# Four durations in the planner of an attention and expert kernel, set to recorded ones

## The chip, the core and the metric

The kernel runs on one core of a Trainium2 chip. The metric is the device time of one execution in microseconds; the time before is the median of three runs. Engines are named as in the profile: PE is TensorE (PEld its weight loads), DVE is VectorE, ACT is ScalarE, POOL is GpSimd, SP is the engine whose queue issues the DMAs.

## What is computed

Rotary attention over 4 x 8 heads of 576 positions with 64 features, then a gated feed-forward layer over the 2304 tokens that come out of it:

```python
q_rot, k_rot = rotate(q), rotate(k)
scores = q_rot @ k_rot.T / sqrt(64)          # per head, 576 x 576
attn = softmax(scores)
x = (attn @ v), as 2304 tokens x 512
xn = x / sqrt(mean(x * x) + 1e-6) * rms_g
h = silu(xn @ w_gate) * (xn @ w_val)         # 512 -> 1536
out = h @ w_out                              # 1536 -> 512
```

## The kernel before

The kernel does not issue its instructions as it comes to them. It first describes them as operations to a planner (`Program`), each with the tiles it reads and writes, one or more engines that may run it, and an assumed duration on each. `order` then plans: `forward` is a list scheduler that fills the five engine queues (A, D, P for ScalarE, VectorE, GpSimd, T for TensorE, S for SP's DMAs) by priority, and chooses the engine of an operation with alternatives by the earliest assumed end; `backward` turns the plan into latest starts, which are the priorities of the next round. There are six rounds, and the plan with the shortest assumed total is emitted. So assumed durations decide two things only: the order in each queue, and the engine where there is a choice. On the chip each engine takes its queue strictly in that order and waits for semaphores.

The assumed durations come from `cost` (lines 384 to 398): a constant and a slope per element. An operation's result counts as there 0.10 us after its end, 0.12 us later on another engine (0.2 on TensorE). Small operations (under 16 elements per partition) have a fixed duration on VectorE, the reciprocal (`recip`) its own. A two-input operation on GpSimd has a slope of 2.15e-3 us per element.

The work has two halves that overlap. Attention goes over 16 pairs of heads (`prep_steps`: load, rope, split into two fp16 parts, transpose by DMA) and, in each, over blocks of 128 queries and one head (144 units in `ORDER`). Of a unit, `scores` runs matmuls into a PSUM tile sc; `softmax` has VectorE scale sc and reduce it to the row's bound (line 655, with an accumulator output), ScalarE take the exponential, ScalarE and VectorE split it into two fp16 parts (hl), and a DMA transpose it (pt); the first 16 units are transposed on TensorE instead (line 470). `pv` multiplies pt by the values into po, and `pv_evac` adds and scales it into xb (or x for the odd 64 rows) with a row sum sm.

The feed-forward half first decodes and splits 18 weight blocks in wall (`decode`, `split_w`, mostly VectorE), which needs no attention, then runs over nine groups of 256 tokens: `mm_in` (twelve matmuls to each half of a PSUM tile mo), `gate` and `hidden` make h and its fp16 parts ht, `mm_out` multiplies by the output weights, and `out_evac` stores. Its matmuls stand last by their first priority (`mo=1000`), so that they fill TensorE where attention leaves it idle.

Operations that may run on VectorE or GpSimd are the three steps of rope on each of q and k (576 elements, into ra, lk, lq), and the last product of `pv_evac` (128 elements, xb or x by sm).

Of the kernel before, what the change touches and what calls it, by code (L numbers as in the profile page):

```python
# [12 lines left out]
ALU = mybir.AluOpType  # L13
AX = mybir.AxisListType
RED = bass_isa.ReduceOp
PSUM = bass.MemoryType.PSUM
# [8 lines left out]
LAST = {}  # L25
# [35 lines left out]
def real(x):  # L61
    return x.ap() if isinstance(x, View) else x


class Program:
# [206 lines left out]
    def order(self):  # L272
        for o in self.ops:
            for n in o.need:
                n.succ.append(o)
        best = None
        LAST["runs"] = []
        for r in range(P["runs"]):
            total = self.forward()
            if total is None:  # L280
                LAST["runs"].append(None)
                break
            LAST["runs"].append(round(total, 1))
            if best is None or total < best[0]:
                best = total, {o: (o.pick, o.eng, o.start, o.end) for o in self.ops}, {h: h.slot for o in self.ops for h in o.held}
            if r < P["runs"] - 1:
                late = self.backward(total)
                for o in self.ops:
                    o.prio = late[o]
        for o, (o.pick, o.eng, o.start, o.end) in best[1].items():  # L290
            pass
        for h, h.slot in best[2].items():
            pass
        done = sorted(self.ops, key=lambda o: (o.start, o.idx))
        LAST.update(ops=done)
        return done
# [3 lines left out]
def rope_attention_then_swiglu_kernel(  # L300
# [18 lines left out]
    nc = tc.nc  # L319
    B, NH, S, D = q.shape  # L320
# [14 lines left out]
    pr = Program()  # L335
# [7 lines left out]
    def ring(name, shape, dtype, bufs=1):  # L343

        if name not in rings:
            rings[name] = [[const.tile(shape, dtype, name=f"{name}{i}") for i in range(bufs)], 0]
        r = rings[name]
        r[1] += 1
        return r[0][(r[1] - 1) % len(r[0])][:]
# [36 lines left out]
    def cost(e, o, ins, two):  # L386
        n = max([o.free_size()] + [x.free_size() for x in ins])
        psum = any(x.space == PSUM for x in ins)
        if e == "A":
            return 0.10 + 0.83e-3 * n, False  # L390
        if e == "D":
            if n < 16:
                return 0.08, not psum and o.space != PSUM
            fast = not two and not psum and o.space != PSUM
            return 0.06 + (0.55e-3 if fast else 1.13e-3) * n, not psum
        if n < 16:
            return 0.15, True
        return 0.08 + (2.15e-3 if two else 1.05e-3) * n, True

    def ts(engs, o, i, s1, op0=ALU.mult, s2=None, op1=None, prio=0.0):  # L400
        r = [i] + [s for s in (s1, s2) if is_ap(s)]
        alts = []
        for e in engs:
            def emit(e=e):
                a = dict(out=real(o), in0=real(i), scalar1=s1, op0=op0, scalar2=None)
                if op1 is not None:
                    a.update(scalar2=s2, op1=op1)
                elif e == "P":
                    a.update(scalar2=1.0, op1=ALU.mult)
                ENG[e].tensor_scalar(**a)  # L410
            alts.append((e, *cost(e, o, [i], False), emit))
        pr.add(alts, [o], r, prio)

    def stt(o, i0, s, i1, op0=ALU.mult, op1=ALU.mult, prio=0.0):
        d, lock = cost("D", o, [i0, i1], True)
        pr.add([("D", d, lock, lambda: nc.vector.scalar_tensor_tensor(out=real(o), in0=real(i0), scalar=s, in1=real(i1), op0=op0, op1=op1))],  # L416
               [o], [i0, i1] + [x for x in (s,) if is_ap(x)], prio)

    def tt(engs, o, a, b, op=ALU.mult, prio=0.0):
        pr.add([(e, *cost(e, o, [a, b], True), lambda e=e: ENG[e].tensor_tensor(out=real(o), in0=real(a), in1=real(b), op=op)) for e in engs], [o], [a, b], prio)  # L420

    def act(o, i, func, scale=None, bias=None, accum=None, prio=0.0):
        def emit():
            kw = {}
            if scale is not None:
                kw["scale"] = scale
            if bias is not None:
                kw["bias"] = bias
            if accum is not None:
                kw["accum_out"] = accum  # L430
            nc.scalar.activation(out=real(o), in_=real(i), func=func, **kw)  # L431
        d = cost("A", o, [i], False)[0] + 0.09 * (is_ap(scale) + is_ap(bias)) + 0.15 * (accum is not None)
        return pr.add([("A", d, False, emit)], [o] + ([accum] if accum is not None else []), [i] + [x for x in (scale, bias) if is_ap(x)], prio)

    def cast(engs, o, i, scale=None, prio=0.0):

        r = [i] + ([scale] if is_ap(scale) else [])
        alts = []
        for e in engs:
            d, lock = cost(e, o, [i], False)  # L440
            if e == "A":
                d += 0.09 * is_ap(scale)

                def emit():
                    nc.scalar.activation(out=real(o), in_=real(i), func=ACTF.Copy, **({} if scale is None else {"scale": scale}))  # L445
            elif e == "D":
                def emit():
                    nc.vector.tensor_scalar(out=real(o), in0=real(i), scalar1=1.0 if scale is None else scale, scalar2=None, op0=ALU.mult)
            else:
                def emit():  # L450
                    nc.gpsimd.tensor_scalar(out=real(o), in0=real(i), scalar1=1.0 if scale is None else scale, scalar2=1.0, op0=ALU.mult, op1=ALU.mult)
            alts.append((e, d, lock, emit))
        pr.add(alts, [o], r, prio)
# [3 lines left out]
        pr.add([("D", d, i.space != PSUM, lambda: nc.vector.tensor_reduce(out=real(o), in_=real(i), op=op, axis=axis, **kw))], [o], [i], prio)  # L457

    def recip(o, i, prio=0.0):
        pr.add([("D", 0.08, False, lambda: nc.vector.reciprocal(o, i))], [o], [i], prio)  # L460

    def fill(engs, o, x):
        pr.add([(e, 0.1 + 1e-3 * o.free_size(), True, lambda e=e: ENG[e].memset(o, x)) for e in engs], [o], [])
# [25 lines left out]
    def transpose(o, i, prio=0.0):  # L489
        pr.add([("S", 1.35, 0.0015 * i.free_size() * i.shape[0] / 128, lambda: nc.sync.dma_start_transpose(out=o, in_=i))], [o], [i], prio)  # L490
# [153 lines left out]
    def softmax(i):  # L644


        u, m, h = ORDER[i]
        p, sc = T[i], U[u]["sc"]
        if h != 1:
            SM[u, m] = ring("sm", [128, 4, 2], FP32, P["sm"])  # L650
        sm, n = SM[u, m], h or 0
        x = p(lambda t: t[:, :, 0:HS])

        d, _ = cost("D", x, [x], True)
        pr.add([("D", d, False, lambda: nc.vector.tensor_scalar(out=real(x), in0=real(x), scalar1=sc[:, 3:4], scalar2=None, op0=ALU.mult, op1=ALU.min, accum_out=sm[:, 0, n:n + 1]))],  # L655
               [x, sm[:, 0, n:n + 1]], [x, sc[:, 3:4]])
        if i < P["nt"]:

            e = ring("hl", [128, 2, S], FP16, P["hl"]).rearrange("p a c -> p (a c)").bitcast(FP32)
            act(e.rearrange("p (c n) -> p c n", c=2), x, ACTF.Exp, scale=-1.0, bias=sm[:, 0, n:n + 1], accum=sm[:, 1, n:n + 1])  # L660
            return turned(i, e)
        stay = i >= P["eps"]
        e = x if stay else ring("e", [128, S], FP32, P["e"]).rearrange("p (c n) -> p c n", c=2)
        act(e, x, ACTF.Exp, scale=-1.0, bias=sm[:, 0, n:n + 1])
        hl = ring("hl", [128, 2, S], FP16, P["hl"])
        hl4 = hl.rearrange("p a (c n) -> p a c n", c=2)
        cast(USE["Hs"] if stay else USE["H"], hl4[:, 0], e, 4096.0)
        stt(hl4[:, 1], e, 4096.0, hl4[:, 0], ALU.mult, ALU.subtract)
        pt = ring("pt", [128, 10, 128], FP16, P["pt"])[:, 0:J]
        transpose(pt, hl.rearrange("p a c -> p (a c)"))  # L670
        T[i] = pt

    def turned(i, e):


        p = Held(PS["sc"])
        mms([(p(lambda t, blk=blk: t[:, blk // 4, blk % 4 * 128:blk % 4 * 128 + 128]), e[:, 128 * blk - 64 * (blk == 4):128 * blk + 128 - 64 * (blk == 4)], eye, None, None) for blk in range(5)], P["tT"])
        et = ring("pt", [128, 10, 128], FP16, P["pt"]).rearrange("p b c -> p (b c)").bitcast(FP32)
        cast(USE["et"], et, p(lambda t: t[:].rearrange("p c n -> p (c n)")[:, 0:640]))
        T[i] = et.rearrange("p (b c) -> p b c", c=128)  # L680
# [380 lines left out]
    i = 0  # L1061
    late[1] = True
    while i < NS + 8:
# [16 lines left out]
        while done < 2 * HS2 * groups:  # L1080
            G, x = divmod(done, 2 * HS2)
# [61 lines left out]
```

## Time and profile before

| what | us |
|---|---|
| median of three runs | 746.55 |
| lowest and highest | 744.01, 747.24 |
| span of the profiled execution | 741.7 |
| TensorE busy | 648.4 |
| VectorE busy | 524.8 |
| ScalarE busy | 420.6 |
| GpSimd busy | 183.5 |

The profile is of one execution; the page gives its time as the span from the first to the last instruction alone, with no total around it. Busy is the time in which an engine has at least one instruction recorded as running. A recorded duration goes from an instruction's recorded start to its recorded end, and recorded durations of one engine can overlap.

### The profile page before, as it was taken

To read this page: it belongs to the slowest core of one execution; us is meant where nothing else is said; L and a number is where in the kernel's file an instruction comes from. 1 tells how busy PE (TensorE), PEld (TensorE's weight loads), DVE (VectorE), ACT (ScalarE), POOL (GpSimd) and SP (SyncE) were. 2 spreads that over 40 slices of the span, in tenths; PEclk is the share of its full clock that TensorE was granted. 3 is DMA by queue.
4 is the path that set the end of the run, shared out by engine and by line. 5 is a ranking of instruction groups with operands and counts; after the bars stand their busy time and mean duration, and the time that the engine had idled before them with its cause. 6 is when DMAs were issued, how large, how long until landed. Compare 5 with 4: busy or idle time off the path is not lost.

```text
span 741.7 us, 14737 instructions
## 1 busy us (share of the span) xinstructions
PE 648.4 (87%) x5558; PEld 494.5 (67%) x5558; DVE 524.8 (71%) x1321; ACT 420.6 (57%) x775; POOL 183.5 (25%) x216
## 2 busy tenths in 40 slices
PE   0077787599777999989999999999999999999997
PEld 0056675388553688658766886787589588586783
DVE  4889998989999897987997789798778322021120
ACT  5356665656787677776766686677565222121220
POOL 3160000224243224141340533425012112021110
PEclk9997655589989999999999999999999999999999
DMA  9979463998986889799899897979964110100001
GB/s 234 299 135 208 130 211 104 192 205 175 196 155 133 188 137 183 144 195 184 127 197 163 178 180 140 189 131 184 162 126 80 37 43 1 29 2 15 15 1 28
DMA packets 235286, 100.76 MB, mean 136 GB/s; under 512 B 214608, under 2 KB 214736, under 8 KB 235216
## 3 DMA queue, kind: packets, MB, share of 16 engines
q1 hardware_dynamic: 235216, 99.83, 67.2%
q8 instruction: 43, 0.70, 0.4%
q14 instruction: 27, 0.22, 0.1%
HBM read 38.45 MB, written 4.72 MB: 58 GB/s over the span
## 4 chain that ended last, share of the span: by engine, by line
PE 62%; DVE 19%; issue 5%; DMA 5%; ACT 4%; SPq 3%; POOL 1%; DVEq 0%; ACTq 0%; POOLq 0%
PE mo L472 45%; PE po L472 9%; PE sc L472 7%; DVE wall L416 5%; DVE sc L655 4%; DVE hl L416 2%; SPq L487 2%; DMA lv<-in_v_dram 1%; DMA lk<-in_k_dram 1%; DVE h L416 1%; PE sc L470 1%; SPq L490 1%; DVE wall L410 1%; DVE vv L416 1%; ACT hl L445 1%
## 5 line engine op out<-in xcount | busy, mean ns | idle before, releaser
L472 PE MATMUL mo<-xn,wall 128*128 128x256 f16 x2592 | 302.8, 274 | 1.6 <-DVE h L416 1.3
L472 PEld LDWEIGHTS <-wall 128*128 128x128 f16 x2632 | 258.2, 99 | 49.5 <-issue 14.5
L472 PE MATMUL mo<-wall,ht 128*128 128x512 f16 x648 | 149.8, 383 | 4.0 <-DVE wall L416 4.0
L655 DVE TENSOR_SCALAR_CACHE_REDUCE sc<-sc,scl 128x576 f32<-128x576 f32 x144 | 116.6, 818 | 13.3 <-PE sc L472 12.8
L431 ACT ACTIVATE sc<-sc,sm 128x576 f32<-128x576 f32 x128 | 90.7, 710 | 58.0 <-DVE sc L655 51.7
L472 PE MATMUL sc<-k,qt 128*128 128x288 f16 (+1 forms) x600 | 94.9, 306 | 26.0 <-DMA k<-k 12.2
L472 PEld LDWEIGHTS <-ht 128*128 128x128 f16 x648 | 63.1, 99 | 74.1 <-issue 7.9
L416 DVE SCALAR_TENSOR_TENSOR hl<-sc,hl 128x576 f16<-128x576 f32 x128 | 95.3, 751 | 22.1 <-ACT hl L445 21.9
L420 POOL TENSOR_TENSOR ht<-h,ht 128x512 f16<-128x512 f32 x54 | 64.1, 1187 | 185.6 <-ACT ht L445 179.0
L416 DVE SCALAR_TENSOR_TENSOR h<-h,mo 128x512 f32<-128x512 f32 x54 | 36.7, 680 | 87.6 <-ACT h L431 87.4
L472 PEld LDWEIGHTS <-pt 128*128 128x128 f16 (+1 forms) x1296 | 69.2, 103 | 25.1 <-issue 12.3
L472 PEld LDWEIGHTS <-qt 128*128 128x128 f16 (+1 forms) x600 | 53.3, 106 | 48.0 <-issue 19.2
L472 PE MATMUL po<-vv,pt 128*128 128x65 f16 (+3 forms) x1242 | 76.7, 211 | 7.6 <-DMA pt<-hl 3.8
L445 ACT ACTIVATE hl<-sc 128x576 f16<-128x576 f32 x128 | 81.4, 646 | 2.0 <-DMA pt<-hl 0.7
L445 ACT ACTIVATE ht<-h 128x512 f16<-128x512 f32 x52 | 32.7, 628 | 55.2 <-DVE h L416 54.9
L416 DVE SCALAR_TENSOR_TENSOR h<-h,gam,mo 128x512 f32<-128x512 f32 x54 | 40.1, 742 | 25.1 <-PE mo L472 25.1
L431 ACT ACTIVATE h<-mo,pg 128x512 f32<-128x512 f32 x54 | 37.0, 686 | 36.4 <-PE mo L472 31.3
L431 ACT ACTIVATE wall<-mo,uo 128x512 f32<-128x512 f32 x18 | 12.3, 685 | 50.4 <-PE mo L472 47.1
L445 ACT ACTIVATE ov<-po 128x128 f32<-128x128 f32 (+1 forms) x72 | 19.6, 274 | 25.8 <-PE po L472 18.9
L420 POOL TENSOR_TENSOR ra<-lk,sin_t 128x576 f32<-128x576 f32 x10 | 14.2, 1422 | 76.0 <-DMA lk<-in_k_dram 75.9
L472 PE MATMUL po<-wall,pt 128*128 128x64 f32 (+5 forms) x174 | 30.1, 340 | 2.7 <-DVE x L420 1.6
L420 POOL TENSOR_TENSOR xb<-xb,sm 128x128 f32<-128x128 f32 x31 | 14.5, 469 | 64.0 <-DVE xb L420 38.3
(140 smaller groups left out, 713.5 us busy)
## 6 DMA issues: line engine op xcount, KB each, us to landing
out_dram<-wall SPq DMA_DIRECT2D x36, 128.0 KB, 2.5
k<-k SPq DMA_DIRECT2D x30, 144.0 KB, 2.7
wall<-in_moe_w_val_dram SPq DMA_DIRECT2D x8, 512.0 KB, 4.7
stg<-in_moe_w_out_dram SPq DMA_DIRECT2D x8, 512.0 KB, 4.6
lk<-in_k_dram SPq DMA_DIRECT2D x13, 288.0 KB, 3.9
lq<-in_q_dram SPq DMA_DIRECT2D x13, 288.0 KB, 3.3
lv<-in_v_dram SPq DMA_DIRECT2D x13, 288.0 KB, 4.9
lv<-in_v_dram SPq DMA_DIRECT2D x13, 256.0 KB, 4.5
```

The source lines that it names most:

```text
L410: ENG[e].tensor_scalar(**a)
L416: pr.add([("D", d, lock, lambda: nc.vector.scalar_tensor_tensor(out=real(o), in0=real(i0), scalar=s, in1=real(i1), op0=op0, op1=op1))], [o ...
L420: pr.add([(e, *cost(e, o, [a, b], True), lambda e=e: ENG[e].tensor_tensor(out=real(o), in0=real(a), in1=real(b), op=op)) for e in engs], [ ...
L431: nc.scalar.activation(out=real(o), in_=real(i), func=func, **kw)
L445: nc.scalar.activation(out=real(o), in_=real(i), func=ACTF.Copy, **({} if scale is None else {"scale": scale}))
L470: nc.tensor.transpose(real(o), a, b)
L472: nc.tensor.matmul(out=real(o), lhsT=a, rhs=b, start=start, stop=stop)
L487: pr.add([("S", 0.57, kb / 300.0, lambda: nc.sync.dma_start(out=o, in_=i))], [] if dram == "o" else [o], [] if dram == "i" else [i], 0.0 i ...
L490: pr.add([("S", 1.35, 0.0015 * i.free_size() * i.shape[0] / 128, lambda: nc.sync.dma_start_transpose(out=o, in_=i))], [o], [i], prio)
L655: pr.add([("D", d, False, lambda: nc.vector.tensor_scalar(out=real(x), in0=real(x), scalar1=sc[:, 3:4], scalar2=None, op0=ALU.mult, op1=AL ...
```

## The change

Four assumed durations are replaced: small operations on VectorE and the reciprocal go from 0.08 to 0.12 us, GpSimd's slope for two inputs from 2.15e-3 to 2.35e-3 us per element, and the softmax reduction on VectorE gets 0.14 us more, for the accumulator read that follows it. The added line in `order` keeps a copy of the first priorities and is read nowhere.

```diff
@@ order
         best = None
+        LAST["prio0"] = [o.prio for o in self.ops]
         LAST["runs"] = []
@@ cost
             if n < 16:
-                return 0.08, not psum and o.space != PSUM
+                return 0.12, not psum and o.space != PSUM
...
         if n < 16:
             return 0.15, True
-        return 0.08 + (2.15e-3 if two else 1.05e-3) * n, True
+        return 0.08 + (2.35e-3 if two else 1.05e-3) * n, True
@@ recip
-        pr.add([("D", 0.08, False, lambda: nc.vector.reciprocal(o, i))], [o], [i], prio)
+        pr.add([("D", 0.12, False, lambda: nc.vector.reciprocal(o, i))], [o], [i], prio)
@@ softmax
         d, _ = cost("D", x, [x], True)
-        pr.add([("D", d, False, lambda: nc.vector.tensor_scalar(out=real(x), in0=real(x), scalar1=sc[:, 3:4], scalar2=None, op0=ALU.mult, op1=ALU.min, accum_out=sm[:, 0, n:n + 1]))],
+        pr.add([("D", d + 0.14, False, lambda: nc.vector.tensor_scalar(out=real(x), in0=real(x), scalar1=sc[:, 3:4], scalar2=None, op0=ALU.mult, op1=ALU.min, accum_out=sm[:, 0, n:n + 1]))],
```

## Rows read from the trace of the kernel before

**Rows 1.** Busy tenths of TensorE and VectorE in 40 equal slices of the span.
```profile
PE   0077787599777999989999999999999999999997
...
DVE  4889998989999897987997789798778322021120
```

**Rows 2.** Stretches: length; busy us of PE, PEld, DVE, ACT, POOL; clock; DMA.
```profile
0.00:50.00 50.00, 12.02 (x46) 8.58 (x47) 35.60 (x78) 23.84 (x49) 20.60 (x26) 1.00 0.96 239
50.00:150.00 100.00, 73.99 (x483) 60.36 (x481) 91.64 (x246) 64.65 (x112) 6.00 (x7) 0.63 0.66 164
150.00:250.00 100.00, 84.21 (x738) 60.85 (x736) 92.26 (x244) 70.54 (x127) 33.60 (x41) 0.91 0.85 171
250.00:575.00 325.00, 315.91 (x3097) 247.09 (x3095) 272.81 (x702) 227.41 (x436) 98.67 (x120) 0.99 0.89 160
575.00:742.00 167.00, 162.28 (x1206) 117.67 (x1203) 32.44 (x54) 34.18 (x54) 24.66 (x22) 1.00 0.08 19
```

**Rows 3.** Chain of waits from 120 to 250 us: start, us, piece.
```profile
152.28 6.39 PE mo L472 x48
```

**Rows 4.** VectorE's groups, 50 to 250 us: busy us, mean ns, idle before.
```profile
L655 DVE TENSOR_SCALAR_CACHE_REDUCE sc<-sc,scl 128x576 f32<-128x576 f32 x48 | 39.1, 818 | 4.3 <-PE sc L472 4.0 <-ACT xs L431 0.2
...
L655 DVE DVE_READ_ACCUMULATOR sc<-sc,scl 128x1 f32 x48 | 6.7, 139 | 0.0
...
L460 DVE RECIPROCAL sm<-sm 128x2 f32<-128x2 f32 x19 | 2.8, 153 | 0.1
...
L420 DVE TENSOR_TENSOR xb<-xb,sm 128x128 f32<-128x128 f32 x5 | 1.3, 278 | 0.0
...
L420 DVE TENSOR_TENSOR lk<-lk,ra 128x576 f32<-128x576 f32 x1 | 0.8, 752 | 0.0
...
L416 DVE SCALAR_TENSOR_TENSOR uo<-so,gm 128x1 f32<-128x1 f32 x1 | 0.1, 131 | 0.0
```

**Rows 5.** VectorE in order of time, 214 to 222.5 us: start, us, operation.
```profile
215.04 0.83 DVE L655 TENSOR_SCALAR_CACHE_REDUCE sc<-sc,scl 128x576 f32<-128x576 f32 x1 [0.43 <-PE sc L472]
...
216.46 0.16 DVE L410 TENSOR_SCALAR rm<-ssq 128x3 f32<-128x3 f32 x1
...
217.00 0.75 DVE L420 TENSOR_TENSOR lk<-lk,ra 128x576 f32<-128x576 f32 x1
217.67 0.15 DVE L420 TENSOR_TENSOR rm<-rm 128x3 f32<-128x3 f32 x1
...
217.81 0.82 DVE L655 TENSOR_SCALAR_CACHE_REDUCE sc<-sc,scl 128x576 f32<-128x576 f32 x1
218.55 0.14 DVE L655 DVE_READ_ACCUMULATOR sc<-sc,scl 128x1 f32 x1
218.55 0.75 DVE L416 SCALAR_TENSOR_TENSOR hl<-sc,hl 128x576 f16<-128x576 f32 x1
...
221.92 1.33 DVE L416 SCALAR_TENSOR_TENSOR rm<-rm 128x3 f32<-128x3 f32 x1
```

**Rows 6.** All engines in order of time, 215.9 to 216.1 us.
```profile
215.96 0.71 ACT L431 ACTIVATE sc<-sc,sm 128x576 f32<-128x576 f32 x1 [0.16 <-DVE sc L655]
```

**Rows 7.** Waits: 50 to 150 us (first two), then 150 to 250 us.
```profile
PE sc L472 <- DVE hl L416: 10.1, 4, 5.0
...
DVE xb L420 <- PE po L472: 5.4, 4, 2.2
...
PE sc L472 <- DVE hl L416: 9.2, 10, 3.2
```

**Rows 8.** GpSimd's groups, 50 to 250 us: busy us, mean ns, idle before.
```profile
L420 POOL TENSOR_TENSOR ra<-lk,sin_t 128x576 f32<-128x576 f32 x3 | 4.4, 1461 | 40.5 <-DMA lk<-in_k_dram 40.5
...
L420 POOL TENSOR_TENSOR lk<-lk,ra 128x576 f32<-128x576 f32 x1 | 1.4, 1407 | 0.1
```

**Rows 9.** GpSimd in order of time, 214 to 222.5 us.
```profile
214.04 2.30 POOL L420 TENSOR_TENSOR ht<-h,ht 128x512 f16<-128x512 f32 x2 [3.02 <-ACT ht L445]
...
221.83 1.40 POOL L420 TENSOR_TENSOR lq<-lq,ra 128x576 f32<-128x576 f32 x1
```

## The prediction

> **What bounds the kernel now.** I read the busy shares in slices first, then five stretches of the span, then the chain of waits for the first expert matmul on it, then VectorE's groups and its order of time in the stretch that is bound by it, and last TensorE's waits. In the slices [rows 1] VectorE is at nine tenths or close to it up to about slice 30 and then falls off, while TensorE stands below nine in most slices before the 14th and at nine in almost every one after it. The stretches give the sizes [rows 2]. Up to 50 us TensorE waits for loads and the first scores. From 50 to 250 us VectorE is busy for 91.64 + 92.26 = 183.9 of 200 us, TensorE for 158.2, and at a granted clock of 0.63 and 0.91: weight decoding and softmax share VectorE, and the expert matmuls (mo) can't start before VectorE has decoded gate and value weights; their first piece on the chain of waits is at 152.28 us [rows 3]. From 250 us TensorE is the bound (315.91 of 325 us busy), and VectorE has 325 - 272.81 = 52 us to spare. After 575 us nothing but mo is left. So an order of instructions can win or lose time mainly between 50 and 250 us; what is lost there moves mo work, and the end, back by as much, because TensorE has only 325 - 315.9 = 9 us to catch up with afterwards.
>
> **The change, part by part.** No instruction is added or taken away. What changes is what the planner believes, and by that the order in each engine's queue and the choice between VectorE and GpSimd for operations that may run on either. The chip's own durations stay, so by itself the change costs 0; its price is that of the new order.
>
> *The reduction (L655).* The planner booked 0.06 + 1.13e-3 x 576 = 0.711 us of VectorE; now it books 0.851. The profile's rows are 818 ns and 139 ns for the accumulator read [rows 4], 0.957 us together, so the new value looks nearer. But recorded durations of successive instructions overlap. The reduction that starts at 217.81 us is followed by the next operation, hl, at 218.55, and its accumulator read has that same recorded start [rows 5]: the pair keeps VectorE for 0.74 us. Against that, 0.711 is 0.03 short and 0.851 is 0.11 long. The latency is no better: the reduction at 215.04 releases ScalarE's exponential at 215.96 [rows 5, 6], 0.92 us after its start. The planner's arrival there was 0.711 + 0.10 + 0.12 = 0.93; it becomes 1.07.
>
> *Small operations and the reciprocal.* Booked 0.08, now 0.12 us. Recorded: 153 ns for the reciprocal, about as much for the rest [rows 4]. Seven in a row, the first at 216.46 us, are over when a wide operation starts at 217.00 [rows 5]: 0.54 us for seven, 0.077 each, while each is recorded with 0.15 to 0.22. In the gap from 217.67 to the reduction at 217.81 two more have 0.07 each. I take 0.07, so 0.08 was 0.01 long and 0.12 is 0.05 long.
>
> [...]
>
> *How much is overbooked from 50 to 250 us.* There are 48 reductions and 162 operations of under 16 elements (46 groups; the largest and the last stand in [rows 4]). New: 48 x 0.11 + 162 x 0.05 = 5.3 + 8.1 = 13.4 us. Old: 48 x -0.03 + 162 x 0.01 = 0.2 us. The old plan ran at VectorE's real pace in this stretch, the new one is laid out for an engine 13.4 / 184 = 7% slower than it is.
>
> *What an overbooked VectorE costs.* Queues are taken in order. The plan puts other work (mo blocks of twelve, transposes on SP's queue) ahead of what it thinks VectorE will not have released yet; VectorE then comes early and finds its next input not made. Its small idle share (200 - 183.9 = 16.1 us) grows. Below, the price is 0, where the order only shifts as a whole; above, it is all 13.4 us, where VectorE is held to the planned pace. Neither end is excluded. No row shows this wait yet, and the nearest, 5.4 us in which xb on VectorE waits for TensorE's po [rows 7], lies between them; I take half, 6.7 us.
>
> *After 250 us* the same error at the same rate is 13.4 x 325 / 200 = 21.8 us, under the 52 us that VectorE has to spare there, and mo covers TensorE: 0. If that cover were gone, the 9 us of TensorE's idle time could double; that is in the range. *Before 50 us* the loads decide: 0.
>
> *GpSimd's price for two inputs.* 576 elements go from 1.318 to 1.434 us booked, 128 from 0.355 to 0.381, 512 from 1.181 to 1.283. Recorded: 1.40 for 576, but 2.30 for two of 512, 1.15 each [rows 9], so there the new value is farther off. GpSimd is dearer by 0.12 for a rope step, while each reduction queued on VectorE makes VectorE's queue longer by 0.14. The two pull against each other, and I take 0. Bounds: at one end all 12 rope steps that GpSimd holds in this stretch ([rows 8] has the first and the last of six groups) go to VectorE, 12 x 0.67 (start to start: 217.00 to 217.67 [rows 5]) = 8.0 us more on the engine that is the bound. At the other, VectorE's one rope step and its five products of xb with sm (recorded 0.75 and 1.3 us [rows 4], less what overlaps: 0.67 and 1.0) go to GpSimd: 1.7 us less.
>
> *Sum.* 741.7 us of span + 4.85 us around it = the median of the three runs, 746.55 us (the profile gives only the span of its own execution, so what lies around it is taken as the difference). 746.55 + 6.7 + 0 + 0 = 753.2 us, slower by 0.9%.
>
> **The rivals.**
>
> *Faster: the overbooking works as padding.* Between 150 and 250 us TensorE stands for 9.2 us at scores whose buffer VectorE's hl has not yet freed, while mo blocks stand behind it in the queue [rows 7]. A plan with a slower VectorE puts more mo ahead of these scores. All of it back gives 746.6 - 9.2 = 737.4, half of it 742. Between 50 and 150 us the same wait (10.1 us) can't be filled, since there is no mo work yet. It decides for faster from 3.7 us recovered net of the loss above. Against it: VectorE is the bound in this stretch, and an earlier mo only helps where the later scores don't starve VectorE.
>
> *No measurable change.* The order stays the same up to the start of mo, because VectorE's own work up to there is fixed, and behind 250 us TensorE has work in any order: 746.6. That the change doesn't do what it says belongs here: the planner keeps the best of six plans, which could be close to the old one. 0.5% (3.7 us) is about what a measurement of this kernel can tell from no change.
>
> *Slower through the choice of engine.* GpSimd's higher price sends rope steps to VectorE in the bound stretch. From six of the 12 on it outweighs 3.7 us; all of them give 746.6 + 8.0 = 754.6, and with the 6.7 us above 761.
>
> *Slower through GpSimd instead.* If six operations go the other way, their runs can hold VectorE up. An operation on three elements took 1.33 us at 221.92, beside a rope step on GpSimd from 221.83, where its like at 217.67 took 0.15 [rows 5, 9]. Six such meetings cost up to 6 x 1.18 = 7.1 us and give back 1.7: 752. [...]
>
> **How the numbers follow.** Slower by the overbooked pace 0.32, by the choice of engine 0.10, through GpSimd's runs 0.04; no change 0.25; faster 0.29. So slower 0.46, same 0.25, faster 0.29, and 753.2 us for the likeliest. The likeliest's own range is 746.6 + 0 to 13.4, 747 to 760. The range for 8 in 10 reaches down to nearly the whole faster case, 737, and up past 761 to the overbooked pace with part of the 9 us after 250 us, 765.
>
> **What would show it.** In the profile after, VectorE should be busy for about the same total but idle for more than 16.1 us between 50 and 250 us, most of it ended by TensorE (sc, po) or ScalarE; the first expert matmul should start later than 152.28 us, and the stretch in which only mo is left should be longer. TensorE's 9.2 us at hl should shrink. If VectorE's idle time stays and mo starts as early, the pace argument is wrong. If GpSimd's count of rope steps moves by six or more, the choice of engine is what decided. The forecast fails above all if the padding lets TensorE fill its 9.2 us: then mo gains between 150 and 250 us and the end comes earlier.

## The result, and the profile after

The changed kernel takes 753.43 us, median of 13 runs, against 744.03 for the kernel before, measured beside it; the ratio is 1.0113 with a 95% interval of 1.0088 to 1.0137. (Ratios here leave out slow executions, such as one of the 13 that took 1657 us, so a ratio can differ from the quotient of two medians, by up to 0.4%.) The forecast was slower, 753.2 us, with 0.9%.

The page after: span, busy times, the slices of TensorE and VectorE, and the granted clock. The last fence is the granted clock before.

```profile
span 749.7 us, 14738 instructions
...
PE 652.5 (87%) x5558; PEld 499.7 (67%) x5558; DVE 531.2 (71%) x1323; ACT 425.3 (57%) x775; POOL 173.5 (23%) x214
...
PE   0176896598856799998999999999999999999997
...
DVE  5899678999988978998887898789787532021130
...
PEclk9995555599966999999999999999999999999999
```

```profile
PEclk9997655589989999999999999999999999999999
```

The span has grown from 741.7 to 749.7 us, by 8.0. Beside [rows 1], VectorE has a dip in slices 5 and 6 (6 and 7 tenths, 9 and 9 before), and TensorE is weak in slices 12 to 14 (5, 6 and 7 tenths; 7, 7 and 9 before). Its granted clock is at five tenths in slices 4 to 8 and at six in 12 and 13 (7, 6, 5, 5, 5 and 8, 9 before).

The five stretches after, with the columns of [rows 2].

```profile
0.00:50.00 50.00, 13.48 (x63) 9.98 (x64) 38.20 (x78) 25.74 (x53) 21.63 (x28) 1.00 0.83 220
50.00:150.00 100.00, 74.06 (x427) 61.27 (x426) 84.21 (x228) 60.91 (x105) 5.03 (x6) 0.53 0.60 158
150.00:250.00 100.00, 77.40 (x739) 60.20 (x738) 91.36 (x248) 71.19 (x129) 33.81 (x45) 0.84 0.90 182
250.00:575.00 325.00, 317.35 (x3031) 243.28 (x3030) 272.04 (x686) 225.27 (x422) 87.72 (x113) 1.00 0.89 157
575.00:750.00 175.00, 170.23 (x1309) 124.94 (x1306) 45.38 (x87) 42.15 (x70) 25.32 (x23) 1.00 0.14 27
```

VectorE from 50 to 250 us: 200 - 84.21 - 91.36 = 24.4 us idle, against 16.1 before; 7.4 of the 8.3 us more are in the first half, up to 150 us. TensorE from 150 to 250 us: 77.40 us busy, against 84.21. From 250 to 575 us TensorE is as full as before (317.35 against 315.91). What it has not done by then stands at the end: 1309 matmuls and 170.23 us after 575, against 1206 and 162.28. These 7.95 us are the growth of the span. Not all of what is left is expert work: 1247 of the 1309 matmuls are on mo, against all 1206 before, so that 41 of the 103 more are of mo and 62 of attention.

VectorE's and TensorE's waits after: first VectorE's from 50 to 250 us (us in total, times, longest), then TensorE's from 150 to 250 us.

```profile
DVE sc L656 <- PE sc L473: 10.5, 17, 2.7
DVE xb L421 <- PE po L473: 7.6, 6, 2.3
DVE wall L411 <- DMA stg<-in_moe_w_out_dram: 2.3, 2, 1.1
```

```profile
PE sc L473 <- DVE hl L417: 15.6, 12, 2.7
```

VectorE's wait for scores was 4.0 us in the stretch before, and is 10.5; its wait for po was 5.4 [rows 7] and is 7.6. TensorE's wait for hl was 9.2 [rows 7] and is 15.6; from 50 to 150 us it fell, from 10.1 [rows 7] to 7.5. Over the two stretches together both engines wait for each other more.

The chain of waits after, from 165 to 260 us (start, us, piece); the loads of output weights into the one staging tile (first and last start) and the first matmul on output weights, each after and then before; and the second load into the staging tile in SP's queue (start, us), after and then before.

```profile
174.11 6.29 DMA stg<-in_moe_w_out_dram
...
205.19 1.24 SPq L491
206.47 1.36 SPq L491
207.89 1.49 SPq L491
209.43 1.28 SPq L491
210.81 1.31 SPq L491
212.24 5.39 DMA stg<-in_moe_w_out_dram
```

```profile
L488 SPq DMA_DIRECT2D stg<-in_moe_w_out_dram x8: 327/344/581, 122.5 to 212.2; - x8
```

```profile
L473 PE MATMUL mo<-wall,ht x648: 376/379/631, 241.2 to 744.9; 128*128 128x512 f16 x162
```

```profile
L487 SPq DMA_DIRECT2D stg<-in_moe_w_out_dram x8: 328/348/529, 117.4 to 192.9; - x8
```

```profile
L472 PE MATMUL mo<-wall,ht x648: 376/379/634, 220.3 to 736.9; 128*128 128x512 f16 x162
```

```profile
140.76 0.52 SPq L488 DMA_DIRECT2D stg<-in_moe_w_out_dram  x1
```

```profile
127.45 0.33 SPq L487 DMA_DIRECT2D stg<-in_moe_w_out_dram  x1
```

The last load of output weights into the staging tile is at 212.24 us; before it was at 192.9. SP's queue takes five transposes just ahead of it, but they are a small part of these 19 us. Of the eight loads into the tile the first is 5 us later than before, the second 13 and the fourth 26 (174.11 us in the chain, 147.7 before): the delay arises between 117 and 174 us. The seventh is 16 us later, so the transposes ahead of the eighth can have added some 4. The tile is free again when VectorE has decoded what is in it, and that is what comes later: the last decoding step of the first load starts at 126.7 us before and at 139.3 after.

The first matmul on output weights follows at 241.2 in place of 220.3 us. Until then TensorE has, in both kernels, nothing of mo to do but the gate and value matmuls of the first group, 288 in all (6 pairs of blocks x 2 x 2 x 12). By 250 us the records have 303 matmuls on mo, against 354. Attention is not behind at that time (52 reductions begun, against 51); it falls behind next, with 59 against 64 by 288 us.

### The profile page after: what moved, and what is told of

Same layout as the page of the kernel before. It is cut to its first block, busy times and chain, and to the rows that moved or that the text cites. A ratio compares the mean times of both kernels' runs of the same rounds, so it can differ in the third digit from the quotient of the medians.

```text
span 749.7 us, 14738 instructions
## 1 busy us (share of the span) xinstructions
PE 652.5 (87%) x5558; PEld 499.7 (67%) x5558; DVE 531.2 (71%) x1323; ACT 425.3 (57%) x775; POOL 173.5 (23%) x214
## 4 chain that ended last, share of the span: by engine, by line
PE 67%; DVE 13%; DMA 9%; ACT 4%; issue 4%; SPq 3%; DVEq 0%; ACTq 0%
PE mo L473 47%; PE po L473 10%; PE sc L473 8%; DVE sc L656 3%; DVE wall L417 3%; DVE hl L417 2%; SPq L491 2%; DMA lv<-in_v_dram 2%; DMA stg<-in_moe_w_out_dram 2%; SPq L488 1%; PE sc L471 1%; DMA k<-k 1%; DMA wall<-in_v_dram 1%; DMA wall<-in_k_dram 1%; DMA pt<-hl 1%
## 5 line engine op out<-in xcount | busy, mean ns | idle before, releaser
L473 PE MATMUL mo<-xn,wall 128*128 128x256 f16 x2592 | 298.8, 273 | 2.5 <-DVE h L417 2.0
L473 PE MATMUL sc<-k,qt 128*128 128x288 f16 (+1 forms) x600 | 100.1, 315 | 41.9 <-DVE hl L417 25.5
L656 DVE TENSOR_SCALAR_CACHE_REDUCE sc<-sc,scl 128x576 f32<-128x576 f32 x144 | 117.5, 820 | 25.4 <-PE sc L473 24.8
L417 DVE SCALAR_TENSOR_TENSOR hl<-sc,hl 128x576 f16<-128x576 f32 x128 | 96.0, 751 | 14.4 <-ACT hl L446 13.9
L473 PEld LDWEIGHTS <-qt 128*128 128x128 f16 (+1 forms) x600 | 55.1, 108 | 66.3 <-issue 37.3
L473 PEld LDWEIGHTS <-pt 128*128 128x128 f16 (+1 forms) x1296 | 71.1, 105 | 17.9 <-DMA pt<-hl 6.9
L417 DVE SCALAR_TENSOR_TENSOR h<-h,gam,mo 128x512 f32<-128x512 f32 x54 | 40.1, 743 | 22.9 <-PE mo L473 22.6
L421 POOL TENSOR_TENSOR xb<-xb,sm 128x128 f32<-128x128 f32 x41 | 18.1, 445 | 75.0 <-DVE xb L421 34.8
L473 PE MATMUL po<-wall,pt 128*128 128x64 f32 (+5 forms) x174 | 34.1, 375 | 1.1 <-DVE x L421 1.1
L446 ACT ACTIVATE ov<-po 128x128 f32<-128x128 f32 (+1 forms) x72 | 19.4, 271 | 22.3 <-PE po L473 13.2
L473 PEld LDWEIGHTS po<-wall,pt 128*128 128x128 f32 (+1 forms) x120 | 28.0, 329 | 1.8
```

What stands on the lines that cost most here:

```text
L473: nc.tensor.matmul(out=real(o), lhsT=a, rhs=b, start=start, stop=stop)
L656: pr.add([("D", d + 0.14, False, lambda: nc.vector.tensor_scalar(out=real(x), in0=real(x), scalar1=sc[:, 3:4], scalar2=None, op0=ALU.mult, ...
```

## The experiments

Three theories stood. **Pace**, that of the prediction: the changed durations book VectorE for more than it is kept, the order is laid out for a slower engine, and time grows with the overbooking. **Engine choice**: GpSimd's higher price moves rope steps to VectorE. **Redraw**, formed on the result: any change of any duration gives another order, and orders differ by about 1% whatever the sign of the change. All runs are of the planner's inputs or its output; what is computed stays. "Before" in each comparison is the kernel before on the same chip.

**Parts alone.**

```diff
 e1_reduction
-        pr.add([("D", d, False, lambda: nc.vector.tensor_scalar(out=real(x) ...
+        pr.add([("D", d + 0.14, False, lambda: nc.vector.tensor_scalar(out=real(x) ...
 e2_small (the reciprocal too)
-                return 0.08, not psum and o.space != PSUM
+                return 0.12, not psum and o.space != PSUM
 e3_slope
-        return 0.08 + (2.15e-3 if two else 1.05e-3) * n, True
+        return 0.08 + (2.35e-3 if two else 1.05e-3) * n, True
```

> Pace theory (an overbooked VectorE lays the order out for a slower engine, so time grows with the overbooking): the reduction alone is about half of what was added, so about half of the 1.1% loss, 0.4 to 0.7% slower than before, VectorE idle some 20 us between 50 and 250 us. Redraw theory (any changed duration draws another order from a spread, whatever its sign): anywhere within 1.2% of before on either side.

> Pace theory: small operations and the reciprocal alone are the other half, 0.4 to 0.7% slower than before. Redraw theory: anywhere within 1.2% of before on either side, and the parts need not add up to the whole.

> Pace theory: GpSimd's price does not touch VectorE's pace, so within 0.5% of before. Engine-choice theory: rope steps move to VectorE between 50 and 250 us, 6 or more, and it is over 0.5% slower. Redraw theory: anywhere within 1.2%.

Measured: 1.0112 (1.0068 to 1.0155), 1.0042 (1.0004 to 1.0079) and 1.0100 (1.0053 to 1.0147). The sum of the parts would be 2.5%, the whole is 1.1%: they don't add. The reduction alone costs as much as everything together, and GpSimd's price alone, for which the pace theory has nothing, costs 1.0%. In that run GpSimd holds 18 rope steps from 50 to 250 us in place of 12, so the dearer engine got more of them; in the changed kernel the count is 12, as before, and VectorE has two products of xb in place of five and no step of xs (which may also run on either engine) in place of one. For that stretch, which it named, the engine-choice theory falls. Outside it the choice did move: over the whole span GpSimd has 50 rope steps on lk, lq and ra before, 40 in the changed kernel and 30 with its price alone, the difference mostly behind 250 us (30, 21 and 11). VectorE has time to spare there, and TensorE's idle time behind 250 us hardly differs (9.1, 7.7 and 10.5 us), so no run shows a price of it.

Of the pace theory's three forecasts of the time only the second came true; the reduction alone came out above its 0.4 to 0.7%, though its interval just reaches down to that, and the price alone clearly above 0.5%. The redraw theory's, within 1.2% on either side, could hardly fail.

**The durations that the trace shows from start to start.**

```diff
 e4_occupied (the reciprocal too)
-                return 0.08, not psum and o.space != PSUM
+                return 0.07, not psum and o.space != PSUM
-        pr.add([("D", d, False, ...
+        pr.add([("D", d + 0.03, False, ...
```

> Small operations 0.07 us, the reduction 0.03 us more than before: the start-to-start times of the trace in place of the recorded durations, GpSimd as before. Pace theory: VectorE is booked as it runs, so no slower than before, at best up to 0.5% faster. Redraw theory: anywhere within 1.2%, slower as likely as faster.

Measured: 1.0104 (1.0067 to 1.0141). VectorE is booked as it runs, and the kernel is as slow as with the change. Its stretches from 50 to 250 and from 250 to 575 us:

```profile
50.00:250.00 200.00, 165.15 (x1205) 127.52 (x1205) 183.14 (x486) 135.71 (x237) 42.09 (x48) 0.89 0.74 166
250.00:575.00 325.00, 307.20 (x2980) 237.30 (x2978) 268.15 (x672) 221.52 (x420) 94.45 (x121) 0.99 0.87 158
```

VectorE is idle for 16.9 us in the first, almost as before; the loss is in the second, where TensorE is idle for 325 - 307.20 = 17.8 us, against 9.1 before. So the pace theory can't explain this loss, and a truer booking by itself gave nothing.

**Hardly a change at all.**

```diff
 e5_jitter_small       small operations: 0.08 -> 0.081
 e6_jitter_reduction   the reduction: d -> d + 0.002
 e7_jitter_slope       GpSimd: 2.15e-3 -> 2.16e-3
```

> Small operations booked with 0.081 in place of 0.080 us: no error of a duration changes to speak of. Pace theory: within 0.5% of before. Redraw theory: the order is another one, and the time can be up to 1.2% off on either side.

> The reduction booked with 0.002 us more (0.713 in place of 0.711). Pace theory: within 0.5% of before. Redraw theory: another order, up to 1.2% off on either side.

> GpSimd's slope for two inputs 2.16e-3 in place of 2.15e-3 (0.006 us on 576 elements). Pace theory: within 0.5% of before. Redraw theory: another order, up to 1.2% off on either side.

Measured (the reciprocal went with the small operations): 1.0070 (1.0035 to 1.0106), 1.0032 (0.9995 to 1.0070) and 1.0119 (1.0060 to 1.0179). A slope changed by half a percent costs as much as the whole change, as near as four executions can tell. This is the redraw theory's case, and it speaks against reading the 1.1% as the price of wrong durations.

**More of it, and the other way.**

```diff
 e8_double    small (reciprocal too) 0.16, reduction d + 0.28
 e12_under    small (reciprocal too) 0.04, reduction d - 0.14, GpSimd 1.95e-3
```

> VectorE's three added durations doubled (small operations and reciprocal 0.16, reduction 0.28 us more; GpSimd as before). Pace theory: slower than the changed kernel by about as much again, 1.8 to 2.5% slower than before, VectorE idle over 30 us between 50 and 250 us. Redraw theory: in the same spread as the others, no more likely beyond 1.2% than they.

> The four durations changed by the same amounts the other way: small operations and reciprocal 0.04, the reduction 0.14 us less, GpSimd's slope 1.95e-3. Pace theory: VectorE underbooked, so it is not slowed to a planned pace, within 0.5% of before or a little slower by TensorE waiting for it. Redraw theory: 0.3 to 1.2% slower, as the other small changes were, or somewhat more, since the durations are off by as much as in the change.

Measured: 1.0309 (1.0238 to 1.0380) and 1.0076 (1.0040 to 1.0111). The doubled overbooking stands clear of the other changes of durations, and its reductions wait longest for TensorE over the whole span (busy us, mean ns, idle before; 12.8 us of it were TensorE's scores before, 24.8 with the change and 21.1 underbooked):

```profile
L655 DVE TENSOR_SCALAR_CACHE_REDUCE sc<-sc,scl 128x576 f32<-128x576 f32 x144 | 117.3, 821 | 41.2 <-PE sc L472 40.3
```

The stretches of the two runs, the doubled one first:

```profile
50.00:250.00 200.00, 150.85 (x1124) 116.44 (x1123) 173.89 (x465) 127.29 (x221) 35.00 (x43) 0.70 0.74 159
250.00:575.00 325.00, 308.63 (x2941) 237.50 (x2940) 262.06 (x664) 221.99 (x418) 107.50 (x132) 0.98 0.88 160
```

```profile
50.00:250.00 200.00, 164.46 (x1245) 130.00 (x1244) 188.88 (x497) 134.59 (x243) 42.10 (x54) 0.81 0.77 167
250.00:575.00 325.00, 311.79 (x3003) 239.77 (x3002) 270.71 (x692) 224.40 (x428) 95.50 (x117) 1.00 0.88 161
```

VectorE's idle time from 50 to 250 us has the ends that the pace theory asks for: 11.1 us underbooked, 16.1 before, 19.7 (e1) and 22.6 (e2) for the parts, 24.4 for the change, 26.1 doubled, though over 30 had been forecast for the last. But GpSimd's price alone (e3), which leaves VectorE's booking as it was, gave 22.9, as much as e2; and two changes of no meaning (e5, e7) gave 13.9 and 14.3. So a step of nearly the size of the change's 8.3 us comes without any overbooking too. And the underbooked plan, with VectorE the fullest of all, is still 0.8% slower. The doubled plan is the one result that the redraw theory, as forecast, does not cover, and it is slower than the pace theory's 1.8 to 2.5% as well; by the quotient of the medians it is 2.7%.

**Where it is lost.** Both plans are made in one kernel; the operations of one up to its 64th reduction (at 287 us in the kernel before, at 302 us in the changed one) are issued in its order, the rest in that of the other, with the engines that each plan chose.

```diff
+        old = self.plan()
+        for o in self.ops:
+            o.alts = [(a[0], getattr(a[1], "new", a[1]), *a[2:]) for a in o.alts]
+        new = self.plan()
+        one, two = (old, new) if HEAD == "old" else (new, old)
+        cut = one[self.marks[CUT]][2] ...        # CUT is 63
+        head = sorted((o for o in self.ops if one[o][2] < cut), key=lambda o: (one[o][2], o.idx))
+        tail = sorted((o for o in self.ops if o not in inside), key=lambda o: (two[o][2], o.idx))
```

> Both plans are made; the order before is issued up to its 64th softmax reduction (some 288 us on the chip) and the rest in the changed plan's order. First-part theory (the loss of the changed kernel arises before 288 us, where its output weights come late): within 0.5% of before. Second-part theory (it arises in the stretch behind, where the orders also differ): about 1% slower than before.

> The mirror image: the changed plan's order up to its 64th reduction, then the order before. First-part theory: about 1% slower, the first matmul on output weights at about 240 us. Second-part theory: within 0.5% of before.

Measured: 1.0068 (1.0031 to 1.0105) with the old head, 1.0124 (1.0059 to 1.0190) with the new one. With the new head the loss is as large as with the whole change: its first matmul on output weights is at 243.8 us, and 298 matmuls on mo are done by 250 us. The old head has 222.3 and 348. Its 0.7% (5.1 us) lies between the two forecasts (within 0.5%, and about 1%) and its interval reaches into both, so the time alone does not decide; the trace shows a place for it. TensorE's longest wait from 280 to 310 us, and the stretches 275 to 300 and 350 to 575 us of this run:

```profile
PE po L522 <- ACT jk L481: 7.2, 1, 7.2
```

```profile
275.00:300.00 25.00, 16.88 (x169) 13.79 (x167) 18.64 (x47) 12.87 (x25) 3.47 (x5) 0.87 0.79 149
350.00:575.00 225.00, 224.86 (x2166) 175.80 (x2165) 183.33 (x461) 151.27 (x282) 59.39 (x75) 1.00 0.87 155
```

At the seam one matmul of a head pair's bounds (po from ACT's jk) holds TensorE's queue for 7.2 us, for a load that the old head had not yet sent for; TensorE is busy for 16.88 of 25 us there, against 24.20 before. The changed kernel has no such stall (its longest wait from 250 to 350 us is for hl, 3.8 us in all), so it belongs to the seam. From 250 to 350 us TensorE does 833 matmuls, against 951 before. Behind it, from 350 to 575 us, it is idle for 0.1 us, against 4.3 before, and does 2166 matmuls, against 2148. So the new order's second part shows no loss of its own behind 350 us, and the first-part theory is the better supported, with two reserves: the seam adds a stall, and no run issues one plan unmixed in this way, so that what the way of issuing costs by itself is not shown (up to 250 us the two heads run much like the kernels that they come from).

**The late weights by themselves.**

```diff
+        if PULL:     # 14.0
+            todo.sort(key=lambda o: (new[o][2] - (PULL if self.wout.get(o, 0) >= 30 else 0.0), o.idx))
```

> The changed plan's order in which 24 operations alone, the last six loads of output weights with their decoding on VectorE, are put 14 us of planned time earlier; VectorE's booked durations stay those of the change. Late-weights theory: the first matmul on output weights comes 10 us or more earlier than 241 us, and 3 to 8 us of the loss come back, 0 to 0.7% slower than before. Pace theory: VectorE's idle time between 50 and 250 us stays at some 24 us and the time within 0.4% of the changed kernel.

Measured: 1.0366 (1.0300 to 1.0431), far off both. The edit did not do what it was for: the first matmul on output weights came at 263.2 us, later still. VectorE's waits from 150 to 250 us in this run say why.

```profile
DVE wall L463 <- DMA stg<-in_moe_w_out_dram: 7.1, 3, 3.5
...
DVE wall L463 <- DMA wall<-in_moe_w_out_dram: 6.1, 1, 6.1
```

VectorE's queue reached decoding steps whose loads had not landed; it stood for 13.2 us at them, and all behind it. Of these, 7.1 us are for loads into the one staging tile, the last of which came at 219.3 us, against 212.2 in the changed kernel. The edit also took hold too late: it moves only the last six of twelve loads, and the delay is there from the third on, which went into the staging tile at 140.76 us, against 127.45 before. Whether earlier weights alone would give the loss back is open.

**All plans side by side**, each number from its run's stretches and from the matmuls on mo in order of time, the last one from its page (times in us).

| run | ratio to before | quotient of medians | VectorE idle 50-250 us | first matmul on output weights | mo matmuls by 250 us | TensorE idle 250-575 us | TensorE busy, whole span |
|---|---|---|---|---|---|---|---|
| before | 1 | 1 | 16.1 | 220.3 | 354 | 9.1 | 648.4 |
| after | 1.0113 | 1.0126 | 24.4 | 241.2 | 303 | 7.7 | 652.5 |
| e1_reduction | 1.0112 | 1.0123 | 19.7 | 218.6 | 354 | 16.9 | 656.1 |
| e2_small | 1.0042 | 1.0073 | 22.6 | 218.5 | 350 | 15.1 | 651.7 |
| e3_slope | 1.0100 | 1.0108 | 22.9 | 234.6 | 318 | 10.5 | 656.0 |
| e4_occupied | 1.0104 | 1.0109 | 16.9 | 226.1 | 342 | 17.8 | 657.2 |
| e5_jitter_small | 1.0070 | 1.0034 | 13.9 | 213.3 | 403 | 15.7 | 645.5 |
| e6_jitter_reduction | 1.0032 | 1.0031 | 16.4 | 211.6 | 372 | 13.5 | 651.8 |
| e7_jitter_slope | 1.0119 | 1.0085 | 14.3 | 235.0 | 312 | 11.2 | 649.3 |
| e8_double | 1.0309 | 1.0267 | 26.1 | 223.2 | 333 | 16.4 | 653.2 |
| e12_under | 1.0076 | 1.0074 | 11.1 | 236.7 | 312 | 13.2 | 655.9 |

Each slower plan shows one of two marks, or both: the output weights come late, so that few mo matmuls are done by 250 us (after, e3, e7, e12), or TensorE has 4 to 9 us more of idle time from 250 to 575 us (e1, e2, e4, e5, e6, e8, e12). The plan before has neither. How long VectorE is idle in the first stretch does not tell which.

These are marks and not full accounts. TensorE's busy time, with the same 5558 matmuls, makes up more than half of what the profiled span has grown in e1, e3, e4 and e12 (spans of 753.9, 753.6, 754.1 and 750.4 us against 741.7), and the marks do not explain it; in the doubled plan (e8, 761.7 us) 7 us more idle time behind 250 us are a third of the growth. Each trace is of one execution, too, while the executions of the kernel before that the ratios use lie between 739.3 and 751.2 us. And the two measures of a ratio differ by up to 0.4%, so that plans nearer to each other than that are not ranked.

## Why the prediction was right, and where its reasons were not

The number, the sign and the stretch were right. The first step, that the change costs nothing by itself and all through the order, holds, and so, as far as the mixed orders show, does the stretch: the loss comes with the new order's part up to its 64th reduction (e10), and TensorE does not catch up with it after 250 us. The end is not put back by mo alone, though, as the prediction had it: of the 103 more matmuls left at 575 us, 62 are of attention.

The step that sized it, "what an overbooked VectorE costs", foretold what VectorE would do, and is wrong as an account of the time. VectorE's idle time from 50 to 250 us was to grow by up to 13.4 us, with half of that as the price; it grew by 8.3 us, most of it ended by TensorE as foretold (sc and po, 9.4 us before and 18.1 after), and the span by 8.0. That the booking made it grow is not shown: GpSimd's price alone, with VectorE's booking as before, made it grow by 6.8 us (e3). The time does not follow the booking, except at twice the overbooking. A plan with VectorE booked as it runs (e4) loses 1.0%, one underbooked loses 0.8%, and the smallest change of GpSimd's price 1.2%. The forecast's agreement to within a microsecond is therefore largely luck, twice over. The sum started from 746.55 us, the median of three runs, while the 13 beside the changed kernel have 744.03; and its price of 6.7 us, itself half of a bound, was 9.4. The two errors cancel. And the plan before stands at the fast end of the plans tried: none of the nine other sets of durations was faster, and only the 0.002 us on the reduction gave an interval that reaches it, so that slower was the likely sign for any change. Why that plan is the fastest no run shows; that the kernel's other settings were chosen with the old durations in place would do it, and is untested.

That is the rival which the prediction lacked: not "no change" and not a mechanism of one duration, but a plan drawn anew, which from this start lost 0.3 to 1.2%, the doubled one apart. As redraw was first put, with either sign as likely, it does not hold either: all ten came out slower, nine of them clear of no change. The runs show two kinds of mark that such a plan bears. In the changed one it is the late output weights, whose loads fall behind between 117 and 174 us, while VectorE's decoding steps stand farther apart (from the first step on the first load to the first on the third it is 36.2 us, from 133.3 to 169.5, against 21.4 before, from 124.0 to 145.4). That the overbooking of VectorE did this, rather than chance, no run shows, and that the late weights are the cause of the whole loss is not shown either, since the run that was to bring them forward did not.

The other steps, point by point. *Recorded durations overlap*: the after profile has the same rows (47 reductions of 819 ns, accumulator reads of 140 ns), so the durations did not change, only their booking; but the inference that the old bookings were better because they were nearer is not borne out by e4. *GpSimd's price, taken as 0*: mis-sized as a part by itself; alone it measured 1.0%, though not through either of the bounds that were worked out, since no step moved to VectorE in that stretch. By the sign given for this rival, a count that moves by six or more, it did move over the whole span, from 50 to 40 rope steps on GpSimd, but behind 250 us, where VectorE has time. The steps that may run on either engine also include the last one of xs, which the description of the kernel leaves out. *After 250 us, 0*: right for the changed kernel (TensorE idle 7.7 us against 9.1), wrong for most of the other plans, where the 4 to 9 us more are lost just there. *The rival "faster"*: TensorE's wait for hl from 150 to 250 us was to shrink and grew from 9.2 to 15.6 us; the padding did not put mo work ahead, because mo had none to give until the output weights were there. *The reading of the slices*: VectorE is at nine tenths or close to it only up to about slice 15, and at seven to nine from there to the 30th; no term hung on it. *What would show it*: the first expert matmul on the chain of waits is later, as said:

```profile
157.47 1.31 PE mo L473 x12
```

It was at 152.28 us [rows 3]. But the first expert matmul of all is hardly later (first and last start, after and then before), so it is not the start of mo that moved but the output weights behind it:

```profile
L473 PE MATMUL mo<-xn,wall x2592: 269/273/283, 153.2 to 729.4; 128*128 128x256 f16 x200
```

```profile
L472 PE MATMUL mo<-xn,wall x2592: 269/273/421, 152.1 to 721.5; 128*128 128x256 f16 x200
```

The stretch of mo alone at the end was to grow; it shrank, because attention itself ended about 19 us later (the last reduction starts at 580.6 us, and at 561.5 before).

## What to carry to other kernels

A planner's assumed durations are inputs of a search, and the smallest change of one draws another plan; before a change of them is credited or blamed, run a few changes of no meaning (a thousandth on a duration) and see how far the time spreads. Here that spread was as large as the effect. A recorded duration need not be what an instruction keeps its engine for (here 0.957 us recorded for the reduction and its read, 0.74 us from start to start): read the booking from the starts of successive instructions. To find where a load falls behind, compare its starts one by one and not the last alone. To see where two orders part in time, issue one up to a cut and the other behind it, and look at the seam first.

## What had not been expected

From 50 to 150 us TensorE is busy for the same 74 us before and after, but with 483 matmuls before and 427 after, at a granted clock that was 0.63 and is 0.53 [rows 2]. From 150 to 250 us it is 0.84 against 0.91. At the lower clock a matmul takes longer: in the changed kernel four score matmuls on 128x288 take 0.92 us from their start to that of the next group at 106.56 us, where the clock is 0.50, and 0.49 at 302.47 us, where it is 1.00. Over the span its busy time rose from 648.4 to 652.5 us with the same 5558 matmuls. So half of the span's 8.0 us shows as idle time of TensorE (741.7 - 648.4 = 93.3 and 749.7 - 652.5 = 97.2 us) and half as busy time, and idle time alone would have told only half. Why the clock was lower is not shown by any run. A lower clock is not what the slower plans share: e4 had 0.89 from 50 to 250 us (0.63 and 0.91 before in its two halves) and lost 1.0%, with 657.2 us of busy time.
